# Another written order of 2400 tasks, and four more idle products, in a fused attention and feed-forward kernel

## The chip, the cores and the metric

The kernel runs on one core of a Trainium2 chip. The engines named below are TensorE (PE; its weight loads are listed apart as PEld), VectorE (DVE), ScalarE (ACT), GpSimd (POOL) and SyncE (SP, which only issues transfers here). The metric is device time in microseconds (us), the median of several runs. A profiled execution gives the trace that is quoted; its own time is given beside its span.

## The reference

Two blocks, one after the other. The first is a linear attention with decay (batch 4, 8 heads, 768 steps, 48 channels a head), the second a feed-forward block on 3072 tokens (384 to 2048 to 384):

```python
for t in range(S):
    kt, vt, rt = (k[:, :, t], v[:, :, t], r[:, :, t])
    cur = np.einsum('bhd,bhe->bhde', u[None] * kt, vt)
    y[:, :, t] = np.einsum('bhd,bhde->bhe', rt, state + cur)
    state = w[None, :, :, None] * state + np.einsum('bhd,bhe->bhde', kt, vt)
...
x = np.ascontiguousarray(attn_out.transpose(0, 2, 1, 3)).reshape(B * S, H * D)
h = x @ w_in
g = h - np.tanh(h)
return (g @ w_out).astype(np.float32)
```

The inputs are float32, but the two weights of the feed-forward block come as 64-bit floats and are converted on the chip.

## The kernel before

**Attention in units.** The 768 steps are cut into 12 chunks of 64, and the four batches into two halves of two; a unit is one chunk of one half, so there are 24 units, numbered chunk by chunk, and unit n needs the state that unit n - 2 left. A unit loads r, k and v (SP, two transfers each; the first two units share them with ACT's queue), transposes r and k on PE into one PSUM tile (L806 and L808: `turn`, `turn_k`), scales them (`rT` on DVE, L660; `kT` on ACT, L692, or on DVE), forms the scores (`lev`, L828, 32 or 64 small products), masks them on DVE (`cp`, L830), adds the diagonal (`rk`, `rk` times u, `du` on DVE, then `diag` on ACT in two halves; for unit 0 alone the diagonal is a product of its own with `kU` and `w_u`), multiplies with v (`out`, L831) and updates the state (`add`, L792, and `decay`). The result goes through ACT to `xt` and `rest` (L765); POOL then issues six small transfers that move `rest` into the free rows of `xt`. Units 0 and 1 have `extra`, a copy on POOL (L739), in its place. Units 12 to 23 take r and k already spread out by SP and transpose them on DVE.

**The feed-forward block in tiles.** Two units make one block of 256 tokens (j = 0 to 11), and 256 columns of w_in make one tile, named j.f with f = 0, 2, ... 14: 96 tiles. A tile is a first layer of two halves on PE (L217; two h buffers in PSUM), five ACT steps (`s` arctan L229, `th` and `tg` tanh L231 and L233, `sq` L224, `small` L235), three DVE steps (`g`, `m`, `cp`, L242 to L246), and a second layer in two halves: plain products (L254) for the first tiles of blocks 0 to 5 and the very last tile, and else seven products of half size in place of eight (L307), for which POOL, or DVE in two of the last tiles, forms three sums of g (L290 to L294). PE runs first layers ahead of second layers by several tiles.

**Weights.** 16 pieces; each is loaded in parts (SP and POOL for w_in, SP for w_out) and converted by five DVE and two ACT instructions (cv0.0 to cv0.6 for piece 0, L185 to L191).

**The order.** The whole program is a list of 2400 tasks with their dependences, made by `add(engine, cost, run, after, ...)`. Which task is written when is not computed: it is read from the string ORDER, two characters of a 64-letter alphabet a task. Each engine and each DMA queue works in the order in which its tasks are written. The numbers from 2400 on stand for idle products, whose result nothing reads, and for the reading of a flag:

```python
idle, done = [run for _, _, runs in self.fills for _, run in runs], set()
for n in (DIGITS.index(x) * len(DIGITS) + DIGITS.index(y) for x, y in zip(ORDER[::2], ORDER[1::2])):
    if n < len(self.tasks):
        t = self.tasks[n]
        assert all(x.n in done for x in t.after)
        done.add(n)
        yield t.run
    else:
        yield (idle + [None])[n - len(self.tasks)]
```

Idle products (L534) come in four kinds: 512 or 256 columns wide ("wide", "narrow"), into an h buffer or into the PSUM tile of the early units' transposes. They multiply the identity with itself. Nothing else in the program depends on ORDER; the costs and due times given to `add` are not used when the order is read from the string.

Of the kernel before, what the change touches and what calls it, by code (L numbers as in the profile page):

```python
# [42 lines left out]

DIGITS = "0123456789ABCDEFGHIJKLMNOPQRSTUVWXYZabcdefghijklmnopqrstuvwxyz+_"
ORDER = (
    "00010J2i2j2k2f2g2h0H2m2l2nbWbW020K030I040605bWbX2q3435362o3231330A2s0F0B0C2r2ubWbX2x072v2y082w2t0T092z0L380M3U3C"
# [4 lines left out]
    "5Q6A8q8Y56696B5R8Z5S5t5A6c578f5E5u5m8g5B5Y8i5v5lba5n595p8j5C8a585D6Z8b5Z8t0u6a6b8k8s5o5w8l6d6e5a8m8c6F5q5b6J8n14"
    "6N6G6H5r5c6O738o5s775d5x8w74755y6P8r8u915z6Q5e76786n8v6K6f8x5+6R6g6h6o6p6I5_926L7T8y7U7V609D7X6M67617W7Y6q6j656S"
    "7H636r0v687A668z6T956494936i98966U7IJx9762JyJz6k7J6V9EJ+6l6W8+J_K06m6X797B9G996s1D9H7h129F6Y9I9A9R907D7K6tKP9S9K"
    "7L7a9L6u9T7i9U7j0G7C0x9J7E6vKL9d7FKMKN0y8_7Z7b7d9e6w9MKOKQ9V726x9B7G6_1L9Y7k6z707M0zK16+719f9C7N9W9h9Z7c9X7e9iKs"
    "9a7O7lKu16K9K2K39N7PKAKvKw6y9O7g7fKrKt7QKZKa9r0+7RKR179g0_7m9Q9P9j9k9b187n10197o119s7p9l1T1U1E9c1F7q1A1G7vA19m7t"
    "9v1B7u1H7xA21C7w9u7y9t9n9yA41e1fKB1V9w1W1I1gKC1h9oLF1JA5LGLHAF9x1M9p1NA3AGA81O9z9qAR9+KDA6ASA7A9AJKb9_AIAAAUAMA0"
    "1PKc1QABAH1RAKAfAL1SATAg1iAVANAWAYAXAC1jADAZ1kArK6AEAaLIAhAsKWAi1xAOAkLJLKAjAPLl1lAmLmLnAnAQAuAvAtAyB3Aw1mAlB4Az"
    "AxLo1KLpLqAbB51XB6AoBFA+B71YB8BABG1Z1n1aBT1oBIBJBBAc2G2HBHL31p2FB9L4BUAdBMBKBCBf1bBWAeL5BVAp1cBYBXBNBgBLBaBbAqBi"
    "LTBh1dA_7S23241q2526B01rMABO1sKSKTB1BtBk1yBj1z1tBuB2Bm1+1uBD1_1vBZBE1wBlBvBcBPBy20KxBxBQBwKyKzBnBz2PB_2EC327B+28"
    "C4Bo29BRCH2A21C7BSCIC52BC6C0BdCK22CJCACLBe2XC82CM9MBCMCTCOC92ICN2DBp2J2QBq2RBr2SCUCPMf2TLzMgMhCBChCWCCCVBsCYCiCQ"  # L60
    "CXKdCbC1N3L+CZN4N52UC2CkCj2VCmCDCl2W2KCaCE2LCoCnCt2M2NCuCcD5CFCxCpCwCvCqD6CyCGC+CRD82OD7CzDK2Y2Z2aDL2bCSD92cDADC"
    "CdDBDDC_DZCfDM2dDNCe2eDaCgDECrD0DcDODFCsDbDRDGDdDPDgDoDQ85De86DpDfDS7rD1DrDhDq87EEDTD3DsDUDiEFDtDVDvD2EHDH81DuDW"
    "89ETEIDjEGELEJEUD4DkEK88EiDwEW8AEVDxDIEXEYDJDXEaDy7sDlEjEMENExEk8BElLUEmEy8CEZLVEnEbDYEoEqEzDmEpEOEcEPFNErE_DzE+"
    "FOF0EQF1D+F3DnFQ82FPD_F2EdFSE1EeFTE2FcF4EfFRE3E4E0FdE5EsE6EtE7ERE8FeEBFfE9FUFhESEuFVFgEDFrECFWF5FjEgF6FsEhFtFvEv"
    "FwFXFuFzFYFiEw7zFxEAG4FyF7FZFkG5Fl83F8FmG684G9FnG8F9F+G7FAGWGB7+FBGXFCFDFEFaFFGYGaFGFKGbGlGCGAFLGZF_FbGdFoGmGeGD"
    "FpFHGnFIGqG0G+GoGcG1FMGpG_GfGE7_FqGFH2GsH0FJG280H1GgGtGrG3GGH3H4GhGHGiGJGKGIGLGMHDGNGOGPHEGQGTGSH6GjK5GuH5HHGvGk"
    "HFH7GwHIHfHGGxHJHKH8HgK4H9GVGyHiHAHhHkGzHjHBHlHnHLKVHuK8HvHmK7I7HxHwI8HMKUHyHNHCH_IAHOHzHPHQH+I0HoKEI1IBHpI9IEIM"
    "ICHqKYGRINHrIFLPGUIoKFIOIQKXIDKGIRIPHRIUL6ITIpK+IGISHSIHKHJ1HTHUIIIVI2KIJ2HVIqKJIJIrHsHWL7HXK_HYHtJ4IsKeJ5IWIvIt"
    "IXIuJGKfI3J3I4L1J6I5LOJ7HZIwJHHbJ8HaIxI6JIL2JLKgJJLuJKKKL0JVLWHcJNJMHeJWJ9IyKhJAIKHdKiLQLMJOLXILKmLvKjIzJZL_IZI+"
    "JYJPIYIbJXIcIaJBJaIdIeJbKpL8IfJcKnKlIgI_MCJCIhL9KqMDMEJQIiJ0JRJdJEJSKoLAMNMjJDMOMiMkJFIkLBIlLSJTImLCInLRPJMJKkPK"  # L70
    "JeMtJfPYPLPNJgPMJUIjPOMIPQJhPZPPPRLDLEPnPaPbPcPoPfLLLNPSLYPqNaMuPrPTNZNbQ0M0PuPULZM1PVQ1MPLxPpPdJiN+PsPgLrPeQFQ3"
    "PhJkQ2JlLaPiQ4JmJnPtPjQ7JjLbLyQGLcJoMpMKQUPvLfQILkPwQHQ5QVPxQJQ8Q6LgPWJpLjQWPyJqQKQMLsLtLhPXQXJrPkMoQLLdPlQZJuQ9"
    "M2LwQYQAMQPmQBMLQaJwP+MRPzMFQbJtN6M3QjLiNzN_MMMGMHM4QcN7N8LeQkM5MqQNQyQmQOQlQPQnQzNcM6QqQQQdQRP_M7R0QCRMQ+JsQ_Qe"
    "QoR3MSJvM8QfRNMsQgQDMvNjMTMwMrQEMxMUQrQpRPQsRbR1QtR2R4NiQSRQQuR5QvQTRTRcR6R7QhReR8NDRORRQiRSRUQwRfRVRdRiRgQxRWRh"
    "RXRqMmRYNdNeRrMlMnS3RsRuRtS4O1MVRxN9RjR9NANBRkNCRBRCSIS7RlRDS5RERvRAS8S6RZMWSARFRwO0O2SJRyNfRGRzNgNhSXRHSMR+NESK"
    "SYRLSLMbS9SPR_RaSBS0MXSmSZMZMYSNMcSCSaRoMdSOSQRJSDSRMyMeRINHSnRmNnOWRnOTRpSoMaOUOVSbRKS1OXOYScSSSeSpSfSTSrS_MzSq"
    "SESdSuSFOrS2SsStSUNFSGSvT0O6NINJTPT1NoT2NpSHSgNGShM+SiTQM_O7SjSVTST3TRSWT6TTT4SkTWNKOBT7NLSlNkOvT5TeTUOsOtT8N0O4"
    "TfTXT9NqOhTtTATVN1SwTiTYTuThTBTgTlTjSxSzTkSyTmTwNMTnTxT+U6U7S+U9UATCTvToUDU8TZNmTyULTaTzT_UBOdUMTbU0TpUaNNUOUNUC"
    "TDTEUQTFUbU1TGO3O5THU2OuOwTITcUdTMUPURUSNOOCTJUpNPTKODTONlTdNQU3OEUqNWN2OcNVUTTqTrUENTP3UcNRTsNrUUU4UFOFNSUVUfOi"
    "U5UsUWUrNsUeUGUtUhTLUJUgNtUHUuUIV2UvUXUxTNOANUUKNXNYV3O9UYUiO+P4UwNuUjUyVSNvOjUzUZV4U+OkUkOaUnO_V6UlOlUmVTU_V5V7"  # L80
    "UoV8VAV0VWV9VVVUOZObVhVZVXVBVYVaViNwVbVwVjVcOxVkOyOzVCVlVxVdVoVeOeV1VDV+NxVyVFVEVzVmVnVpOGV_W0W2W9VHW1VGW3O8WAVI"
    "VJOHWOVqNyWDVrOgOIWCWBP5WPVKVLVMVfVOWQVNW4WEOJVgW5WHVsVuOfOKVtWSORVvWGP6OOOLOQWdP7OMVQP0VRWTW7OPWRW6WFW8WIWeWVWJ"
    "WKOmWfOSWgWLWhVPWsP1WtOnP2OoWvWkWMOpWWWNWUOqWXX5WuWYWwP8WiWZWzWjWaONX6WxP9WlWbX8WmWyW+WnX9PAX7XCW_WcPBXVPCXAXWPD"
    "PIPFXkXYWoXZPHXBWpXlXcPEXXXDX0XzXnXaWqXbXdXEWrXoXFXmX3XGXpX1XqXsXHX+XrX2XtPGYCY0XeX_Y2XfX4Y1YDY4XuY5XgXIYGXvYFXh"
    "XKYRYJYEXwYHY3XJYKYIXLYSXMXNYLXiY6YTYVY7YgYUYWYYYXXOYhXPXSXQXRYvY8YjXTYkY9YiXjYlXxYmYnYMYZXUYwYNYaYOYoXyYxYzYpZ8"
    "YyYbZ0Z9YcYdYAZBY+ZCZYZ1ZAZDYBY_ZZZFYqZ2YrZnZGZcYsZbYPZEZaZHZdYQZeZoZfZ3Z4YeZpZ5ZqZrYfZsa0ZtZuZIZvZJYtZwZgYuZhZ6"
    "Zia1aFa2a5aGa4a3a6a7Z7aJa8aIaUZxaMZyZLZzZKZNZjZOaVa9ZkZPZMZQaXaHZlZRaAaKZSaLZVaNajaYZUaOaWaBabaZakaCZTZWZmalanZ+"
    "aaaPamZXayaQaqaRacazadbIa+b0a_Z_bJb3aeafaDagbLaoapaEarb1asaSb2bKaTbNbMahbObPb4aib5atawb6aubQavaxb7bRb9b8bBbCbAbD"
    "bEbSbFbGbHbUbTbV"
# [1190 lines left out]
```

## Time and profile before

| what | value |
|---|---|
| time, median of 3 runs (lowest to highest) | 581.05 us (579.9 to 581.28) |
| profiled execution | 582.91 us, its span 581.2 us |
| busy: PE, DVE, ACT, POOL | 563.5, 432.1, 404.1, 202.5 us |
| granted TensorE clock, mean | 0.994 |
| first-layer products, L217 | 1152 passes, 269.0 us busy |
| second-layer products, L307 and L254 | 994 and 200 passes |
| bytes moved | 38.48 MB, most of it in the first 120 us |

A busy PE in this profile is a PE with a pass under way; the ends of passes are modelled, and a float32 product is recorded as two passes. Idle time is put down to the engine or transfer whose semaphore came last before the instruction. Times in rows are from the start of the span.

### The profile page before, as it was taken

The page shows a single profiled execution, that of the slowest core. Times are in us where ns is not written, and L with a number is a line of the kernel's source. Part 1 is how long each engine was busy: PE and PEld are TensorE (multiplying, and loading weights), DVE is VectorE, ACT ScalarE, POOL GpSimd, SP SyncE. Part 2 cuts the span into 40 slices and gives each one's busy share as a digit, 9 for nine tenths or more (in the row PEclk, how much of TensorE's full clock was granted, in tenths as well). Part 3 has the DMA queues.
Part 4 walks back from the last instruction along what each step waited for, and adds up shares of the span by engine and source line. Part 5 has one row for each costly group of instructions (what it writes and reads, how often), then busy time and mean ns, then how long its engine had stood idle before and what let it go on. Part 6 is the DMA issues. An engine that isn't in the chain of part 4 may idle for free.

```text
span 581.2 us, 14164 instructions
## 1 busy us (share of the span) xinstructions
PE 563.5 (97%) x5487; PEld 481.5 (83%) x5487; DVE 432.1 (74%) x720; ACT 404.1 (70%) x926; POOL 202.5 (35%) x366
## 2 busy tenths in 40 slices
...
GB/s 130 162 204 137 125 100 189 103 76 167 114 120 15 1 1 12 17 55 41 40 74 86 62 94 39 72 86 39 25 50 60 16 34 7 3 29 2 14 16 32
DMA packets 138548, 38.48 MB, mean 66 GB/s; under 512 B 130760, under 2 KB 132904, under 8 KB 138472
## 3 DMA queue, kind: packets, MB, share of 16 engines
...
q14 instruction: 31, 0.25, 0.1%
...
## 4 chain that ended last, share of the span: by engine, by line
PE 79%; DMA 1%; ACT 1%; POOL 0%; DVE 0%; issue 0%; DVEq 0%; POOLq 0%
PE h L217 39%; PE p L307 28%; PE o L254 7%; PE yk_ps L606 5%; DMA xt<-rest 1%; PE p L254 0%; ACT xt L765 0%; POOL xt L786 0%; ACT rest L765 0%; ACT kT L692 0%; DVE rk L696 0%; DVE state L792 0%; DVE last L265 0%; PE x_ps L606 0%; DVEq L696 0%
## 5 line engine op out<-in xcount | busy, mean ns | idle before, releaser
L217 PE MATMUL h<-xt,w_in_sb 128*128 128x256 f32 x1152 | 269.0, 381 | 0.4 <-DMA xt<-rest 0.2
L217 PEld LDWEIGHTS h<-xt,w_in_sb 128*128 128x128 f32 x1152 | 214.8, 190 | 33.1 <-DVE w_in_sb L191 0.9
L290 POOL TENSOR_TENSOR sg<-g 128x256 f32<-128x256 f32 x69 | 55.9, 811 | 200.8 <-DVE g L246 147.0
L242 DVE TENSOR_TENSOR g<-h,th 128x512 f32<-128x512 f32 x96 | 65.8, 686 | 61.8 <-ACT tg L233 20.7
L229 ACT ACTIVATE s<-h 128x512 f32<-128x512 f32 x96 | 57.1, 595 | 54.5 <-PE h L217 40.0
L244 DVE TENSOR_TENSOR tg<-s,tg 128x512 f32<-128x512 f32 x96 | 71.7, 751 | 31.2 <-ACT s L224 27.7
L307 PE MATMUL p<-mixed,sg 128*128 128x192 f32 x426 | 93.0, 327 | 0.0
L246 DVE COPY_PREDICATED g<-small,tg 128x512 f32<-128x512 int32 x96 | 74.3, 783 | 12.6 <-ACT small L235 9.9
L231 ACT ACTIVATE th<-h 128x512 f32<-128x512 f32 x96 | 56.8, 593 | 35.0 <-PE h L217 34.7
L307 PEld LDWEIGHTS p<-mixed,sg 128*128 128x128 f32 x426 | 73.5, 190 | 1.4
L233 ACT ACTIVATE tg<-h 128x512 f32<-128x512 f32 x96 | 56.6, 592 | 22.9 <-DVE g L246 13.3
L307 PE MATMUL p<-w_out_sb,g 128*128 128x192 f32 x284 | 69.9, 328 | 0.0
L235 ACT ACTIVATE small<-s,smallb 128x512 f32<-128x512 f32 x96 | 68.5, 720 | 1.2
L254 PE MATMUL o<-w_out_sb,g 128*128 128x384 f32 x192 | 67.2, 489 | 0.1
L224 ACT ACTIVATE s<-s 128x512 f32<-128x512 f32 x96 | 60.1, 630 | 1.1
L786 POOL DMA_DIRECT2D xt<-rest x66 | 32.6, 498 | 68.9 <-ACT rest L765 68.4
L307 PEld LDWEIGHTS p<-w_out_sb,g 128*128 128x128 f32 x284 | 51.1, 190 | 2.7
L254 PEld LDWEIGHTS o<-w_out_sb,g 128*128 128x128 f32 x192 | 35.9, 190 | 19.4 <-issue 0.2
L704 ACT ACTIVATE at<-same,du 128x64 f32<-128x64 f32 x184 | 47.7, 340 | 5.0 <-DVE du L700 4.8
L292 POOL TENSOR_TENSOR sg<-sg,g 128x128 f32<-128x128 f32 x69 | 39.9, 581 | 3.6
L294 POOL TENSOR_TENSOR sg<-sg,g 128x128 f32<-128x128 f32 x69 | 38.1, 559 | 3.0
L307 PE MATMUL p<-w_out_sb,sg 128*128 128x192 f32 x142 | 34.9, 328 | 0.0
...
## 6 DMA issues: line engine op xcount, KB each, us to landing
...
```

The lines of the kernel that those rows point to most:

```text
L217: self.nc.tensor.matmul(t.h2[:, z], self.w_in_sb[:, t.f // 2, kk, z * 128 : (z + 1) * 128], self.xts[t.j][:, kk].rearrange("p b t -> p (b ...
L224: A.activation(t.s, t.s, AF.Square, scale=G3)
L229: A.activation(out, t.h, AF.Arctan, scale=G2)
L231: A.activation(out, t.h, AF.Tanh)
L233: A.activation(out, t.h, AF.Tanh, scale=G1)
L235: A.activation(out, t.s, AF.Relu, bias=self.smallb, scale=-1.0)
L242: V.tensor_tensor(t.g, t.h, t.th, ALU.subtract)
L244: V.tensor_tensor(t.tg, t.s, t.tg, ALU.mult)
L246: V.copy_predicated(t.g, t.small.bitcast(I32), t.tg)
L254: self.nc.tensor.matmul(self.outs[i], t.g2[:, z, i * C : (i + 1) * C], self.w_out_sb[:, t.f + z, :], start=t.first and z == 0, stop=t.last ...
L290: add(t.s4[:, :2], g[:, 0::3], g[:, 1:2].to_broadcast([128, 2, C]), ALU.add)
L307: self.nc.tensor.matmul(ps[bank][:, half * n : (half + 1) * n], a, b, start=t.first and half == 0, stop=t.last, skip_group_check=True)
```

## The change

ORDER is replaced as a whole. The tasks, their dependences, tiles and buffers are the same 2400. The string has 2420 entries in place of 2416: three more wide idle products (one into an h buffer, two into the transposes' tile) and one more narrow one (into an h buffer), 19 in place of 15. On each engine part of the tasks change place: PE 273 of 462 (by at most 8 places), ACT 514 of 653 (at most 35), DVE 551 of 688 (at most 35), POOL 290 of 337 (at most 16), SP 136 of 188 (at most 30).

The head of the diff:

```diff
 ORDER = (
-    "00010J2i2j2k2f2g2h0H2m2l2nbWbW020K030I040605bWbX2q3435362o3231330A2s0F0B0C2r2ubWbX2x072v2y082w2t0T092z0L380M3U3C"
-    "2+2p0N37393A3G2_3V3W0O3E0U3H3S3I3B3J3D3R3T3F0P3KbWbWbX3L0V3u3b300S3MbX3c3v3w0Q3N3a3f3s3O3g3P3r3t3e0R3Y3Q3hbX8D0w"
...
+    "00010J2f2g2h2i2j2k2l2m2n0HbWbW020K030I040605bWbW2obX2q3534363231332s2t2r070F0A383739bWbX2x0B0C2u082y09bX2v0LbX3C"
+    "3B3U0M3V3W2w0N0U2pbW2z3R0O3G3A3H2+3I2_3F3S3T0V3E3J0T3D3u3K0PbW3L3v3w3b303MbX3c0S0Q3N3r3f3a3s3t3O3g3e3P0R3Y3Q3h3X"
...
 )
```

Decoded and split by engine, the first stretch reads as follows (- before, + after). Names in brackets carry the unit or the tile j.f; ha and hb are the halves of a first layer, oa and ob of a plain second layer, pa and pb of one with seven products; fill is an idle product into an h buffer, xfill into the transposes' tile (w wide, n narrow); state is the state's product of units 0 and 1; rku is rk times u; dga and dgb are the halves of the diagonal; W1.2 is part 2 of weight piece 1, k3.1 the second transfer of unit 3's k, st and xt the transfers out and into xt.

```
PE   -: fill.w fill.w cols fill.w fill.n turn_k(0) turn(0) fill.w fill.n lev(0) own(0) table out(0) turn_k(1)
        turn(1) state(0) fill.w fill.w fill.n lev(1) fill.n turn_k(2) out(1) turn(2) state(1) fill.n ha(0.0)
        lev(2) hb(0.0) turn_k(3) out(2) bound turn(3) xfill.w ha(0.2) lev(3) xfill.w out(3) turn_k(4) turn(4)
        hb(0.2) xfill.n lev(4) xfill.n turn(5) out(4) turn_k(5) oa(0.0) ob(0.0)
PE   +: fill.w fill.w cols fill.w fill.w turn(0) fill.n turn_k(0) fill.w fill.n lev(0) table fill.n own(0)
        fill.n turn_k(1) fill.w out(0) turn(1) state(0) fill.w lev(1) fill.n turn_k(2) out(1) turn(2) state(1)
        fill.n ha(0.0) lev(2) hb(0.0) turn(3) bound out(2) turn_k(3) xfill.w xfill.w xfill.w xfill.n lev(3)
        ha(0.2) out(3) turn(4) turn_k(4) hb(0.2) xfill.n lev(4) xfill.w out(4) turn_k(5) turn(5) oa(0.0)
        ob(0.0)
ACT  -: rows k0.1 r0.1 v0.1 ups k1.1 r1.1 keeps kU(0) doubled downs v1.1 xt(0) cv0.2 cv0.3 dga(1) dgb(1)
        add(0) xt(1) kT(2) add(1) dga(2) dgb(2) cv1.2 cv1.3 s(0.0) dga(3) xt(2) kT(3) rest(2) dgb(3) tg(0.0)
        cv2.2 cv2.3 sq(0.0) dga(4) xt(3) rest(3) kT(4)
ACT  +: rows r0.1 k0.1 v0.1 ups k1.1 r1.1 doubled keeps v1.1 kU(0) downs cv0.2 cv0.3 xt(0) dga(1) dgb(1)
        add(0) xt(1) kT(2) add(1) dga(2) dgb(2) cv1.2 cv1.3 tg(0.0) dga(3) xt(2) kT(3) rest(2) dgb(3) s(0.0)
        cv2.2 cv2.3 sq(0.0) dga(4) xt(3) rest(3) kT(4)
DVE  -: now now now kT(0) rT(0) cp(0) diag(0) cv0.0 cv0.1 kw(0) rk(1) kT(1) rku(1) du(1) kw(1) rT(1) cv0.4
        kw(2) cp(1) cv0.5 rk(2) rku(2) cv0.6 du(2) rT(2) cv1.0 kw(3) cv1.1 rk(3) cp(2) rku(3) du(3) cv1.4
        cv1.5 flagged cv1.6 rT(3) cv2.0 add(2) cv2.1 rk(4) kw(4) rku(4) cp(3) du(4) cv2.4 decay(2) cv2.5 kw(5)
        rT(4) add(3) m(0.0) cv2.6 cp(4) g(0.0) rk(5) cp(0.0)
DVE  +: now now now kT(0) rT(0) cp(0) cv0.0 kw(1) cv0.1 diag(0) kw(0) rk(1) rku(1) du(1) kT(1) rT(1) cv0.4
        kw(2) cp(1) cv0.5 rk(2) rku(2) cv0.6 du(2) rT(2) kw(3) cv1.0 cv1.1 rk(3) cp(2) rku(3) du(3) cv1.4
        cv1.5 rT(3) cv1.6 cv2.0 flagged add(2) cv2.1 rk(4) kw(4) rku(4) cp(3) du(4) cv2.4 cv2.5 decay(2) kw(5)
        rT(4) add(3) cv2.6 m(0.0) cp(4) g(0.0) cp(0.0)
SP   -: rows W0.2 k0.0 r0.0 W0.0 v0.0 k1.0 r1.0 ub k2.0 v1.0 k2.1 W1.2 r2.1 r2.0 k3.0 W1.0 k3.1 r3.1 r3.0 v2.1
        v2.0 k4.1 W2.0 k4.0 r4.0 r4.1 v3.1 v3.0
SP   +: rows W0.2 r0.0 k0.0 v0.0 W0.0 k1.0 r1.0 ub v1.0 k2.0 k2.1 W1.2 r2.0 r2.1 k3.0 k3.1 W1.0 r3.0 r3.1 v2.1
        v2.0 k4.1 W2.0 k4.0 r4.0 r4.1 v3.1 v3.0
POOL -: W0.3 W0.1 w_u now extra(0) W1.1 extra(1) W1.3 W4.3 W5.3 xt xt xt xt xt xt W5.1
POOL +: W0.3 W0.1 extra(0) w_u now extra(1) W1.3 W1.1 W4.3 W5.3 W4.1 xt xt xt xt xt xt W5.1
```

Later places that the text below refers to, again before and after:

```
PE   -: ... ob(5.6) ha(1.10) hb(1.10) ha(1.12) pa(0.8) pb(0.8)    (hb(1.8) stands ahead of ob(5.6))
PE   +: ... ob(5.6) hb(1.8) ha(1.10) hb(1.10) ha(1.12) pa(0.8) pb(0.8)
PE   -: ... hb(11.10) pb(11.0) pa(11.2) ha(11.12) hb(11.12) ha(11.14) pb(11.2) hb(11.14) pa(11.4) pb(11.4) ...
PE   +: ... hb(11.10) pb(11.0) ha(11.12) hb(11.12) pa(11.2) pb(11.2) ha(11.14) pa(11.4) hb(11.14) pb(11.4) ...
DVE  -: ... rku(11) du(11) cv4.0 rT(10) cv4.1 kw(11) cp(2.2) add(9) g(3.0) cp(10) m(3.0) cp(3.0) cv5.0 ...
DVE  +: ... rku(11) du(11) kw(11) cv4.0 cv4.1 m(2.2) cv5.0 rT(10) add(9) rk(12) decay(9) cp(10) cp(2.2) ...
```

The end of PE's list, from pa(11.6) on, is the same in both.

More of the change, by code (lines that the diff above doesn't have):

```diff
@@ L45 @@
 ORDER = (
-    "00010J2i2j2k2f2g2h0H2m2l2nbWbW020K030I040605bWbX2q3435362o3231330A2s0F0B0C2r2ubWbX2x072v2y082w2t0T092z0L380M3U3C"
-    "2+2p0N37393A3G2_3V3W0O3E0U3H3S3I3B3J3D3R3T3F0P3KbWbWbX3L0V3u3b300S3MbX3c3v3w0Q3N3a3f3s3O3g3P3r3t3e0R3Y3Q3hbX8D0w"
-    "3d3i0W3k3X3Z3_3j0X4P430Y8E0d3l4O4Q0Z444L40458F4M4N3m0a463y0D0b3+3n0E0c423o41bY8P150e473x3z3p4p0f8H484Z4o4q0g4V4a"
-    "0h494l8I4bbY4A4R0i4c4m4n4W3q4B4U0j4S4T8Q4v0l4C4X5I4Y4J4D4d8L4K5GbZ4e4I0k5J5K8R4F8G5F5H4f4H8J4G8KbZ4u8S134g4z8U8M"
-    "8T4+4w4s4h0m8N4_4x4i8O4E5i4y4j5j5k500n525P4r4t8V4k5f8d8W515T0t0o5U8e536C0p5V5g5h8p8X5W5M0q6D6E5X540r8h5O0s555L5N"
@@ L51 @@
[L51 to L89, printed above, removed]
+    "00010J2f2g2h2i2j2k2l2m2n0HbWbW020K030I040605bWbW2obX2q3534363231332s2t2r070F0A383739bWbX2x0B0C2u082y09bX2v0LbX3C"
@@ new lines @@
+    "3B3U0M3V3W2w0N0U2pbW2z3R0O3G3A3H2+3I2_3F3S3T0V3E3J0T3D3u3K0PbW3L3v3w3b303MbX3c0S0Q3N3r3f3a3s3t3O3g3e3P0R3Y3Q3h3X"
+    "3ZbX8D0w3d3i3_3k3j0W4P0X8E430d0Y3l4O4Q0Z444L3+454M4N0D8H3m0a463y400b3n41420c3o0e3x3z15470E3p4p0u0fbYbYbYbZ488F4o"
+    "4q4Z0g4V4a8P4m0h494b8I4l4n4A0i4c4S4U0j4B4R4T4W3q8Q5J4v4C4X4Y0l4H4D4d5I5K0k4IbZ4e4K5G8G8L4F5F5H8J4f4J8S4G8KbY4g8T"
+    "138M8R4z4w4h4E4u8N4+4x4i5j0m8O8U4_4r4y4j4s4t500n528X5g515T8d5i5k5U0o535f5h8e0p8W5L5V8V0q8p5M5N8g6D5W0r6C6E545P5X"
+    "8Y695Q550s5O6A6B8q5m5R564k5t8Z5l5n5S5C578h6d5E5u8f5B6Z5p5Y8i5D8k8j5A6cba6e5v8a595Z5w6G8l6a6b8b5a8m8t148c5o5b6J6F"
@@ new lines @@
+    "6H5q6N768n585s5r5c738o8s77785d5x6O5y8w8r6P74758u915z6f6Q8x6g6h8v5e5+6n7X6R8y6K7W7Y5_6I926L7U606o7T7V9D6p796M6461"
+    "94666j6q6S65J+676r7A7B688z6T63J_K093620t966U0v95976k7D6V6i7Z989E6l7a7b6W7HJy8+129F6XKO999I9R6m7I9G7J9A7K6sJxJz6Y"
+    "7h0GKPKQ7L9S6t1D8_9H7E9U6u9K9T7i907C7j9W9d7d9VKL0x6vK10y9B9LK2K36w16KMKN9e7F7G727k6x6z1LK96+7M6y7l70719C9J7N6_9X"
+    "9M7O0z9Y9Z0+7e7c7P9N7fKr9a7QKu9OKAKvKw9g0_9PKsKt9f9rKB7g7R9QKZ9h7m1710189b7n19Ka9i117o9j1A1U9s7p1W9k1B9c7q9l9t7u"
+    "A11E9w7t9m9x7w1F7xA29vKb7v1G1C7y9n9u1M1e1f1H1g1N1h9oA41V9yLFA51I9pAF1T1OA8KS9zA3KRKTAG1P9+A6AR1QA7A99qASKCAALGLH"
@@ new lines @@
+    "1RAH9_AJL3AK1SAIA0AV1J1xAT7SABKDAM1iAUAfAW1jANADKx1kAgAYLmALLlLnACAXAOAi1KAjAr1l1X1pAZAhAsAmAk1mKcB3AaAtAnAEB4Aw"
+    "1YAlKWAPL4AuAv1ZAQAy1aAbAx1bB6BFAzB5AoB8BG1nB7B9A+AcBIBABJAdBTBMBHBBBKBUBCBL1cBfBV1dAeBWBg1oBXBYL52FApK6BZ2H1qBi"
+    "LI26BNAqLJLK241r25Bb1s23A_BO2GBhBa2EBjB01tB1Bm1yBt1zB21+Bu1u1_1vBDBvBcBk20BEByBx1wBlC3BnBw2P27LpC421LoLqBoM9BP28"
+    "MAMBB+29BQB_2ACHBz2BC6BRC7CIBS2CBdCKC0LTCLBe22C5C8CA2XBpC9MgCOCJMfMh2DBqCM2ICNCPCT2J2QCU2RCQ2SLzCh2KBrN3Bs2TCiCB"
+    "KyKzN4N5CCCVC12UCXCW2VC2Ck2LL+CaCDCl2WCYCjCECoCm2MCZCtCpCn2NCu2OD5CGCwCFKdCbCRCcCvCy2YD62ZCqCSD8CxCzC+CdD9C_2aDK"
```

28 lines of the change are left out of this document (added).

## The prediction

> **What bounds the kernel now.** I read the page first, then busy time by stage, then the waits of TensorE, then single engines in order of time where something waits. The page begins:
>
> ```profile
> span 581.2 us, 14164 instructions
> ```
>
> Cut where the character of the work changes, the stage table (span, then busy time of PE, PEld, DVE, ACT, POOL, then granted clock, DMA share, GB/s) is:
>
> ```profile
> 0.00:33.50 33.50, 26.20 (x451) 17.42 (x451) 21.91 (x42) 15.64 (x40) 9.81 (x39) 0.95 0.94 158
> 33.50:50.00 16.50, 13.31 (x310) 9.53 (x302) 14.38 (x25) 15.62 (x47) 3.43 (x7) 1.00 0.78 166
> 50.00:117.00 67.00, 65.83 (x1112) 49.66 (x1110) 58.68 (x101) 64.19 (x184) 14.13 (x29) 1.00 0.66 132
> 117.00:573.00 456.00, 455.75 (x3625) 403.79 (x3625) 335.18 (x552) 308.67 (x658) 175.12 (x291) 1.00 0.25 46
> ```
>
> Four stages, four limits. Up to 33.5 us loads set the pace (DMA share 0.94) and PE is padded with idle products. From 33.5 to 50 ScalarE does: 15.62 of 16.50 us. From 50 to 117 PE (65.83 of 67.00) and ACT (64.19) are both nearly closed. From 117 to 573 PE idles 0.25 us in 456. So the last and by far the longest stage has nothing to give: another order of the same matmuls can only open a gap there. What an order can win lies before 117 us and in the tail. The two rows at the head of PE's waits (total, number, longest):
>
> ```profile
> PE yk_ps L606 <- DVE state L792: 2.0, 2, 1.7
> PE x_ps L656 <- issue: 1.6, 2, 0.8
> ```
>
> The largest single one, 1.7 us, is for the state update of unit 2. "issue" is a wait for nothing that the profile shows; no order aims at it.
>
> **Part 1, before 33.5 us: the loads and POOL's queue.** In the new order POOL takes `w_u` (L564) after `extra` of unit 0 (L739), and one load of weight piece 1 goes behind `extra` of unit 1. POOL, then ACT, in order of time:
>
> ```profile
> 8.46 0.20 POOL L564 TENSOR_TENSOR w_u<-saved 128x4 f32<-128x4 f32 x1 [1.84 <-ACT saved L563]
> ...
> 12.81 0.26 POOL L739 COPY extra<-vt 128x96 f32<-128x96 f32 x1 [2.90 <-DMA vt<-in_v_dram]
> ...
> 20.20 0.26 POOL L739 COPY extra<-vt 128x96 f32<-128x96 f32 x1 [6.43 <-DMA vt<-in_v_dram]
> ```
>
> ```profile
> 9.90 1.28 ACT L709 ACTIVATE kU<-kT,w_u 128x128 f32<-128x128 f32 x4 [1.59 <-DVE kT L665]
> ```
>
> POOL works in order, so `w_u` now waits for v of unit 0. If v lands as before, `kU` starts at 12.81 + 0.26 + 0.20 = 13.3 instead of 9.9: 3.4 us late, and behind it in ACT's queue are w_down and the first xt, and on DVE the diagonal of unit 0 and both kw. v is issued one place earlier on SP, which can take part of this back. The cover lies in waits of DVE that follow:
>
> ```profile
> DVE rk L824 <- DMA ub<-in_u_dram: 1.1, 1, 1.1
> DVE power L185 <- DMA st<-in_moe_w_in_dram: 1.0, 1, 1.0
> DVE smallb L1233 <- PEq L1263: 0.9, 1, 0.9
> DVE kw L807 <- issue: 0.8, 1, 0.8
> DVE rk L696 <- DMA rt<-in_r_dram: 0.8, 1, 0.8
> ```
>
> Without the one of smallb, which comes before all this, they sum to 1.1 + 1.0 + 0.8 + 0.8 = 3.7 us, more than 3.4. The load that moves back on POOL goes out just behind the 20.20 row, one issue later than the load of the same piece that stands there already; kw of unit 3 now comes ahead of that piece's conversion and uses its wait of 1.0 us. I take 0. Bounds: +3.4 with no cover; -1.7, if the clock that this stage lost (0.05 of 33.5 us) is all kept and all on the path. The order of PE changes too (transposes and idle products between the first two units), inside the same waits.
>
> [...]
>
> **Part 2, the idle products.** 19 in place of 15: three wide (512 columns) and one narrow (256) more. PE around unit 3's scores:
>
> ```profile
> 33.73 0.66 PE L656 MATMUL x_ps<-ident,rt 128*128 128x128 f32 x4
> 34.22 1.02 PE L534 MATMUL x_ps<-ident 128*128 128x512 f32 x2
> ...
> 38.59 0.69 PE L606 MATMUL yk_ps<-rT,state 48*64 48x64 f32 x32 [1.69 <-DVE state L792]
> ...
> 50.21 2.75 PE L254 MATMUL o<-w_out_sb,g 128*128 128x384 f32 x8
> ```
>
> A wide one takes 1.02 us, a narrow one no more: 3.1 to 4.1 us of PE time if nothing hides it. What hides it: the waits for loads in the first 20 us, and the 1.69 us here, where three wide and one narrow in a row now stand in place of one wide and the first half of a dense tile. Without that cover it costs all 3.1 to 4.1. I take 0 on top of part 3.
>
> **Part 3, 33.5 to 50 us: the table load and the chain to unit 3's scores.** ACT, then DVE:
>
> ```profile
> 32.25 1.28 ACT L229 ACT_TABLE_LOAD   x1 [1.86 <-PE h L217]
> 33.54 0.60 ACT L229 ACTIVATE s<-h 128x512 f32<-128x512 f32 x1
> ...
> 36.77 0.86 ACT L765 COPY rest<-yk_ps 64x64 f32<-64x64 f32 x4
> ...
> 39.11 0.92 ACT L187 ACTIVATE power<-power,p_bias 128x768 uint32<-128x768 uint32 x1
> ```
>
> ```profile
> 34.32 0.96 DVE L191 TENSOR_TENSOR w_in_sb<-w_in_sb,power 128x768 f32<-128x768 f32 x1
> 36.91 0.69 DVE L660 TENSOR_TENSOR rT<-x_ps,power 128x512 f32<-128x512 f32 x1 [1.63 <-ACT kT L692]
> ...
> 37.98 0.55 DVE L792 TENSOR_TENSOR state<-yk_ps,state 128x384 f32<-128x384 f32 x1
> ```
>
> rT of unit 3 waits 1.63 us until ACT's kT, written ahead of it and reading the same PSUM tile, has ended. In the new order rT is written first and can run when its transposes are done, at about 34.4. ACT's first function of a dense tile becomes tg (tanh) instead of s (arctan); the table load at 32.25 stands directly ahead of the first arctan. If the table already loaded serves tanh, tg starts at 32.25, rest of unit 2 ends at 32.25 + (36.77 + 0.86 - 33.54) = 36.3 instead of 37.6, and the state update follows at about 36.7 instead of 37.98. The four idle products run from 33.73 + 0.66 = 34.4 to 37.5 or 38.5, say 38.0, and are then what the scores wait for: some 0.6 us earlier than 38.59.
>
> Most of it does not stay. The load only moves behind the second half of unit 3's diagonal, where s now is. From the start of s to the conversion at 39.11 are 5.57 us of gapless ACT work; 32.25 + 5.57 + 1.28 = 39.1 in either order, and ACT is closed after it. What can remain is the idle time that ACT still has in this stage, 16.50 - 15.62 = 0.9 us. I take -0.25, nearer to nothing than to all of it. Bounds: 0, and -1.1 if PE carries the stage (1.69 less 0.6).
>
> [...]
>
> **Part 4, 50 to 117 us.** Both engines closed, the same work. PE idles 67.00 - 65.83 = 1.2 us, of which an order may win all or add as much. 0, bounds -1.2 and +1.2.
>
> **Part 5, 117 to 573 us.** The visits of PE to attention work are as many as before, 24. What costs is a dense tile whose first layer follows the one two before it with a single first layer between, since there are two h buffers. Before has one such place; PE, then ACT:
>
> ```profile
> 489.78 6.90 PE L217 MATMUL h<-xt,w_in_sb 128*128 128x256 f32 x30
> ```
>
> ```profile
> 494.47 0.60 ACT L229 ACTIVATE s<-h 128x512 f32<-128x512 f32 x1 [0.20 <-DVE g L242]
> ```
>
> 30 passes take 6.90 us from the first start to the last end. s ends at 495.07, 5.3 us after that start; by then, at 6.90 / 30 = 0.23 us a pass, 23 passes have gone, and the next tile's come right after it. So PE waited here by a fraction of ACT's 0.20; I price the place at 0.25 us. The new order has three (tiles 1.8, 6.14, 10.4): +0.5, and since in two of them ACT takes th, tg and s in one row, I take +0.25. Bounds 0 and several times that, since the stage has no other reserve.
>
> **Part 6, the tail.** DVE, then PE's weight load:
>
> ```profile
> 569.60 0.28 DVE L294 TENSOR_TENSOR sg<-sg,g 128x128 f32<-128x128 f32 x1
> ...
> 569.94 0.30 PEld L307 LDWEIGHTS p<-w_out_sb,sg 128*128 128x128 f32 x2 [0.24 <-DVE sg L294]
> ```
>
> The three sums of that tile (11.10) now come ahead of the next tile's instead of alternating with them. I take -0.2; bounds -0.24 and +0.6, as the last tile's first layer comes one half (1.3 us) later against the end.
>
> **Sum.** 0 + 0 - 0.25 + 0 + 0.25 - 0.2 = -0.2 us. The profiled execution took 582.91 us, 1.7 of it around the span of 581.2; in its terms 582.7. The median of the runs shown, 581.05, is 1.86 below the profiled one; in its terms 580.85, and I say 580.9. About 0.3% (1.74 us) is what a measurement of this kernel can tell from no change.
>
> **Rivals.** *The early gain stays* (faster). The scores of unit 3 come up to 1.1 us earlier, ACT makes room because its order meets PE's better, the 1.2 us of part 4 go too, and the tail gives 0.2: 581.05 - 2.5 = 578.55. For it: DVE's wait of 1.63 us comes from the written order alone and goes; against it: ACT closed from 33.5 to 117. Chance 0.34.
>
> *The late stage spends its reserve* (slower). With PE at 455.75 of 456, any place where a first layer follows too closely on a used buffer opens a gap that nothing gives back. At 0.25 us each it decides from seven such places; ten give 581.05 + 2.5 = 583.55. For it: the old order met hardly any gap in this execution; against it: I find three tight places among 96 tiles. Chance 0.17.
>
> *POOL's queue is not covered* (slower). 3.4 us less only the 1.1 us wait for ub: 583.35. It decides when the weights and r that DVE waits for come early. Chance 0.09.
>
> *The reordered tanh costs a third table load*: if the table taken for tanh lacks arctan, ACT pays 1.28 us more in a closed stage: 582.3, within the bound. Chance 0.04.
>
> The forecast, no change that can be told: 0.36, its own range 579.3 to 582.8. Faster 0.34, within 0.3% 0.36 + 0.04 = 0.40, slower 0.17 + 0.09 = 0.26. The range, 577.8 to 584.3, reaches 0.75 us past either rival's time (the bounds of parts 1 and 5 go farther) and leaves about 2 in 10 out.
>
> **What would show it.** Right: rT of unit 3 without a wait for kT; the table load directly ahead of an arctan and behind unit 3's diagonal; unit 3's scores at 37.5 to 38.5; the first second-layer product, at 50.21 before, within 0.5 us of that; PE idle under 1 us from 117 to 573. Wrong: that product more than 1.5 us from its place (parts 1 to 3), or PE idle of 2 us or more in the long stage (part 5).

## The result

The changed kernel takes 586.31 us (median; 585.52 to 586.87) beside 580.47 us (579.02 to 581.28) for the kernel before in the same comparison: a ratio of 1.0102 with a 95% interval of 1.0077 to 1.0128. Compared again on another occasion it was 587.38 beside 580.25, 1.0122 (1.0092 to 1.0153). The forecast was 580.9, no change. The profiled execution of the changed kernel took 586.87 us, its span is 585.2 us, against 582.91 and 581.2 before. The spans are thus 4.0 us apart where the medians are 5.8: the profiled execution of before was 2.4 us above its median, and a dip of its clock, told of further down, is about 1.7 of that.

PE's waits on the page's waits view (total, number, longest) put the loss in one place. The first three rows after:

```profile
PE h L217 <- DMA xt<-rest: 4.0, 2, 2.1
PE yk_ps L606 <- issue: 1.8, 1, 1.8
PE yk_ps L606 <- DVE state L792: 1.6, 1, 1.6
```

A wait of PE for the small transfers from `rest` to `xt` was 0.2 us before. In the changed kernel this is the chain of waits from 107 us on (start, duration, what; the view ends at 125 us and cuts its last piece there):

```profile
107.79 0.23 ACT rest L765
108.01 0.28 issue
108.29 2.12 POOL xt L786 x4
110.41 7.64 DMA xt<-rest
118.05 0.14 issue
118.19 6.82 PE h L217 x18
```

POOL issues the six transfers of tile block 5 at once when ACT has written `rest`, but the one that PE waits for needs 7.64 us to land. The median over the whole kernel (row of L786, issue to landing, minimum, median, maximum) is nearly the same before and after, and the longest differs; before, then after:

```profile
DMA to landing us min/median/max: 1.6/2.2/5.7
```

```profile
DMA to landing us min/median/max: 1.6/2.3/7.8
```

PE in order of time around the first tile of block 5 (tile 5.0), before and then after:

```profile
113.47 2.74 PE L254 MATMUL o<-w_out_sb,g 128*128 128x384 f32 x8
116.05 1.03 PE L217 MATMUL h<-xt,w_in_sb 128*128 128x256 f32 x4
117.32 4.55 PE L217 MATMUL h<-xt,w_in_sb 128*128 128x256 f32 x20 [0.25 <-DMA xt<-rest]
121.71 4.03 PE L254 MATMUL o<-w_out_sb,g 128*128 128x384 f32 x12
```

```profile
110.73 2.75 PE L254 MATMUL o<-w_out_sb,g 128*128 128x384 f32 x8
115.43 0.67 PE L217 MATMUL h<-xt,w_in_sb 128*128 128x256 f32 x2 [1.95 <-DMA xt<-rest]
118.19 7.68 PE L217 MATMUL h<-xt,w_in_sb 128*128 128x256 f32 x22 [2.09 <-DMA xt<-rest]
125.70 4.03 PE L254 MATMUL o<-w_out_sb,g 128*128 128x384 f32 x12
```

Ahead of tile 5.0 the new order is 113.47 - 110.73 = 2.74 us ahead; behind it, it is 125.70 - 121.71 = 3.99 us late. Of this swing of 6.73 us, 1.95 + 2.09 - 0.25 = 3.79 are the waits. Nearly all of the rest is speed: the same 24 passes take 0.67 + 7.68 = 8.35 us in place of 1.03 + 4.55 = 5.58, which is 2.77 us more. The table by stage shows why, before and after. Its last three columns are the granted clock, the DMA share (the time that packets took, as a share of the core's 16 DMA engines) and GB/s:

```profile
112.00:118.00 6.00, 5.75 (x23) 4.04 (x22) 5.56 (x8) 5.79 (x15) 3.11 (x7) 1.00 0.72 148
118.00:124.00 6.00, 6.00 (x26) 4.61 (x26) 4.65 (x8) 5.97 (x15) 0.00 (x0) 1.00 0.70 100
```

```profile
112.00:118.00 6.00, 2.15 (x7) 0.87 (x5) 5.45 (x9) 5.97 (x12) 0.42 (x1) 0.90 1.19 177
118.00:124.00 6.00, 5.82 (x15) 4.67 (x16) 4.02 (x6) 1.85 (x6) 0.00 (x0) 0.53 0.77 188
```

The clock fell while PE stood still and stayed low when it went on: in slices of 1 us it is 1.00 up to 116 us, 0.91 in the next, 0.50 in the six from 117 to 123, and 0.68 in the one after. PE works again from 118.19; the 4.81 us up to 123 at 0.50 and the next at 0.68 come to 4.81 x 0.50 + 0.32 = 2.7 us of full speed lost, which accounts for the 2.77. The DMA engines were at 1.19 in place of 0.72. The rest of the span adds little: the last products of the kernel start at 572.65 and 577.13,

```profile
572.65 2.74 PE L254 MATMUL p<-w_out_sb,g 128*128 128x384 f32 x8
```

```profile
577.13 2.74 PE L254 MATMUL p<-w_out_sb,g 128*128 128x384 f32 x8
```

4.48 us apart, so 0.49 us were lost after tile 5.0, and from there to the end of the span it is 8.55 us before and 8.07 after. -2.74 + 6.73 + 0.49 - 0.48 = 4.0, the difference of the spans.

**What fills the DMA engines.** SP's queue, before and after (issue times; the transfers to `st` are weight loads of 288 KB each):

```profile
112.85 1.28 SPq L171 DMA_DIRECT2D st<-in_moe_w_in_dram  x3
```

```profile
107.75 1.29 SPq L171 DMA_DIRECT2D st<-in_moe_w_in_dram  x3
109.09 0.60 SPq L644 DMA_DIRECT2D rt<-in_r_dram  x1
109.74 0.62 SPq L171 DMA_DIRECT2D st<-in_moe_w_in_dram  x1
```

POOL's, before and after:

```profile
110.67 2.89 POOL L786 DMA_DIRECT2D xt<-rest  x6 [1.65 <-ACT rest L765]
```

```profile
108.29 3.08 POOL L786 DMA_DIRECT2D xt<-rest  x6 [3.25 <-ACT rest L765]
```

Before, one load of piece 8 goes out at 107.97 and the other three (pieces 8 and 9) from 112.85 on, behind five of the six small transfers; the sixth, the one that PE waited 0.25 us for, took 4.11 us to land. After, all four, 1.15 MB, go out from 107.75 to 110.36, ahead of and among them. A load of piece 9 waits for the staging buffer that the sixth conversion step of piece 5 (cv5.5, L190) frees; the two rows are of DVE, before and after:

```profile
111.84 0.94 DVE L190 SCALAR_TENSOR_TENSOR power<-st,power 128x768 uint32<-128x768 uint32 x1
```

```profile
106.75 0.94 DVE L190 SCALAR_TENSOR_TENSOR power<-st,power 128x768 uint32<-128x768 uint32 x1
```

111.84 + 0.94 = 112.78 and 106.75 + 0.94 = 107.69, each less than 0.1 us ahead of its load. In the string the loads of piece 9 stand behind the small transfers in both orders. That binds nothing here: they are on different queues, and the two times just given show SP going when its buffer is free.

### The profile page after: what moved, and what is told of

Its sections match the earlier page's. It is cut to its first block, busy times and chain, and to the rows that moved or that the text cites. A ratio compares the mean times of both kernels' runs of the same rounds, so it can differ in the third digit from the quotient of the medians.

```text
span 585.2 us, 14166 instructions
## 1 busy us (share of the span) xinstructions
PE 569.6 (97%) x5495; PEld 484.6 (83%) x5495; DVE 432.9 (74%) x720; ACT 404.9 (69%) x926; POOL 204.1 (35%) x366
## 4 chain that ended last, share of the span: by engine, by line
PE 80%; ACT 7%; DVE 5%; DMA 4%; issue 2%; POOL 1%; ACTq 0%; DVEq 0%; POOLq 0%
PE h L217 39%; PE p L307 27%; PE o L254 7%; PE yk_ps L606 5%; DMA xt<-rest 2%; DMA rt<-in_r_dram 2%; ACT at L704 1%; ACT xt L765 1%; ACT rest L765 1%; POOL xt L786 1%; PE h L534 1%; DVE tg L244 1%; PE x_ps L656 0%; DVE g L242 0%; PE p L254 0%
## 5 line engine op out<-in xcount | busy, mean ns | idle before, releaser
L217 PEld LDWEIGHTS h<-xt,w_in_sb 128*128 128x128 f32 x1152 | 217.4, 192 | 37.1 <-issue 2.6
L290 POOL TENSOR_TENSOR sg<-g 128x256 f32<-128x256 f32 x69 | 54.7, 795 | 189.2 <-DVE g L246 134.7
L244 DVE TENSOR_TENSOR tg<-s,tg 128x512 f32<-128x512 f32 x96 | 69.9, 731 | 35.1 <-ACT s L224 20.5
L786 POOL DMA_DIRECT2D xt<-rest x66 | 32.6, 498 | 79.6 <-ACT rest L765 79.3
L292 POOL TENSOR_TENSOR sg<-sg,g 128x128 f32<-128x128 f32 x69 | 42.6, 620 | 3.2
L294 POOL TENSOR_TENSOR sg<-sg,g 128x128 f32<-128x128 f32 x69 | 38.5, 563 | 3.7
L307 PE MATMUL p<-mixed,g 128*128 128x192 f32 x142 | 34.8, 327 | 0.1
```

The source lines that it names most:

```text
L217: self.nc.tensor.matmul(t.h2[:, z], self.w_in_sb[:, t.f // 2, kk, z * 128 : (z + 1) * 128], self.xts[t.j][:, kk].rearrange("p b t -> p (b ...
L244: V.tensor_tensor(t.tg, t.s, t.tg, ALU.mult)
L290: add(t.s4[:, :2], g[:, 0::3], g[:, 1:2].to_broadcast([128, 2, C]), ALU.add)
L307: self.nc.tensor.matmul(ps[bank][:, half * n : (half + 1) * n], a, b, start=t.first and half == 0, stop=t.last, skip_group_check=True)
```

## The experiments

Times are medians, beside the kernel before in the same comparison (579.63, 580.25, 580.64 and 580.99 us in the four groups); ratios carry their 95% interval. Edits are given as differences of an engine's list, in the names of the change.

### Is it the loads? Taking them away from the changed kernel

e1_w9_later and e2_w8_first leave every instruction of the engines where the changed kernel has it and move only loads on SP:

```diff
 SP  r14.1
-W9.0 W9.2
 W8.2 r15.0 W8.0 v13.1 v13.0 r15.1 W11.0
+W9.0 W9.2
 v14.0
```

```diff
 SP  r14.1
+W8.2 W8.0
 W9.0 W9.2
-W8.2
 r15.0
-W8.0
 v13.1
```

> The changed kernel with two entries of SP's list moved: the two large loads of weight piece 9 go behind the load of piece 11, so those of piece 8 go out some 4 us earlier and those of piece 9 behind the six transfers of tile 5's rest. Theory C (the loads of pieces 8 and 9, 1.15 MB issued at 107.75 to 110.36, crowd out the small transfers that move rest into xt): these transfers land within about 2.5 us of their issue, PE's two waits of 1.95 and 2.09 us ahead of tile 5 and the clock dip after them go, 586.3 - 6.7 = 579.6 us (579.0 to 580.5). Rival L (the new order lets PE reach tile 5 too soon after its transfers are issued, whatever else moves): waits and time stay, 586.3.

> The changed kernel with the two large loads of weight piece 8 written ahead of those of piece 9 on SP, nothing else. Piece 8 then goes out when its staging buffer is free, about 103.4, and only piece 9 (0.58 MB instead of 1.15) stands at 107.75, ahead of the six transfers. Theory C: about half of the delay is left, PE waits 0.5 to 2 us ahead of tile 5, 580 to 583.5 us. Rival L: 586.3.

e1: 585.7 beside 579.63, 1.0092 (1.0056 to 1.0127). The total was missed by 6 us, but not for the reason that rival L gave: the waits for xt are gone. PE's and DVE's waits in it have another name:

```profile
PE h L217 <- DVE g L242: 3.6, 2, 3.3
```

```profile
DVE power L185 <- DMA st<-in_moe_w_in_dram: 5.2, 1, 5.2
```

The conversion of piece 9 stands on DVE where it stood; its load now comes 13 us later, DVE waits 5.2 us in front of it, and the `g` behind it in DVE's queue holds up PE. I had moved the transfer and not asked who waits for it.

e2: 582.35, 1.0038 (1.0010 to 1.0065), inside the expected 580 to 583.5: with half of the bytes ahead of the small transfers about two thirds of the loss is gone. Its profile has a wait for xt of 0.8 us, but it is of the fastest of twelve executions, at a clock of 1.000 where their median is 0.996, so it need not be typical.

e5_no_block adds to e1 the other half of the move, on DVE. On ACT it also moves the third step of the same conversion (cv9.2) four places back, behind the two tanh of tile 0.4:

```diff
 DVE decay(10) g(5.0)
-cv9.0 cv9.1
 m(5.0) g(5.2) cp(5.0) cv6.6 cv8.0
+cv9.0 cv9.1
 m(5.2) g(0.4)
-cv9.4
 cp(5.2) m(0.4) cv8.1 kw(13) rku(14)
+cv9.4
```

> The changed kernel with the loads of piece 9 behind that of piece 11, as in the first experiment, and with the first two conversion steps of piece 9 on DVE behind the first step of piece 8 (and its fifth step three places later), so that DVE does not stand before a load that has not landed. Theory C+ (the loss is the collision at tile 5 plus the clock dip that PE's standing still brings, and the new order is otherwise even with the old one): neither the wait for xt nor the wait for g, 578.5 to 580 us beside a kernel before of about 579.6. Rival M (part of the loss sits in the rest of the new order): 581.5 or more.

582.96 beside 580.25, 1.0034 (1.0016 to 1.0053). The two thirds of the loss are gone again, yet 2.7 us stay (2.0 by the ratio): too much for C+, and what M expected. Part of it can be named, and it is of my making, not the new order's: DVE still waits 1.06 us for the load of piece 9, and PE 2.1 us for `g`:

```profile
PE h L217 <- DVE g L242: 2.1, 2, 1.8
```

### Putting the stall into the kernel before

e3_before_w9_early moves two conversion steps on DVE, which frees piece 9's buffer early:

```diff
 DVE cp(11) cv4.5
+cv5.4 cv5.5
 cv4.6 m(3.2) cv6.0 cv6.1
-cv5.4
 cp(3.2)
-cv5.5
 cv5.6 g(4.0)
```

> The kernel before with two DVE instructions moved: the fifth and sixth steps of the conversion of piece 5 come right behind the sixth step of piece 4, so the staging buffer of piece 9 is free at about 109.8 instead of 112.8 and its loads go out ahead of and among the six transfers of tile 5's rest (issued from 110.7) instead of behind them. Theory C: the stall appears in the kernel before: 580.5 + 4 to 6.7 = 584.5 to 587 us, with a PE wait for xt of 2 us or more near 116. Rival L: 580.5, no such wait.

585.36 beside 579.63, 1.0092 (1.0064 to 1.0121). Two instructions of one engine, moved by five places at most, cost as much as the whole change. SP now issues four loads in one row ahead of the small transfers, PE waits 2.1 us, and a transfer takes up to 6.5 us to land:

```profile
104.42 3.46 SPq L171 DMA_DIRECT2D st<-in_moe_w_in_dram  x4
```

```profile
PE h L217 <- DMA xt<-rest: 2.1, 1, 2.1
```

Rival L falls: PE is ready for tile 5.0 at 112.67, 5.5 us after the first of its transfers is issued (107.13); before it was 116.05 - 110.67 = 5.4 us.

### The clock's share

```diff
             t.h = t.h2.rearrange("p z t -> p (z t)")
+        for _ in range(10 if (t.j, t.f, z) == (5, 0, 0) else 0):
+            self.nc.tensor.matmul(t.h2[:, z], self.w_in_sb[:, 0, 0, :128],
+                                  self.xts[t.j - 1][:, 0].rearrange("p b t -> p (b t)"), start=True, stop=True)
         for kk in range(d.NK):
```

> The changed kernel with ten idle products (0.43 us each, 4.3 us) ahead of tile 5's first product, into the h buffer that it is about to fill; they take the place of the two waits of 1.95 and 2.09 us. If the clock of 0.5 to 0.8 from 115 to 124 us is a consequence of PE standing still, it stays at 1.00 and the 2.7 us that it cost go: about 583.6 us. If the dip has another cause, 586.3.

584.32 beside 579.63, 1.0075 (1.0049 to 1.0101); the changed kernel stands at 1.0102 and 1.0122, so 0.27 to 0.47% (1.6 to 2.7 us) are back, although PE does 4.3 us of products for nothing (from 111.59 to 115.91 in its profile). The intervals of the ratios overlap, so the size of this gain is only roughly known. The mean clocks do not overlap: 0.996 to 0.999 in its eight executions, 0.987 to 0.994 in the changed kernel's nine. Behind the idle products PE still waits 1.1 us for xt. In its profile the clock stays at 1.00 through the stall:

```profile
112.00:118.00 6.00, 4.93 (x23) 4.05 (x22) 5.43 (x9) 5.00 (x11) 0.00 (x0) 1.00 1.11 158
118.00:124.00 6.00, 6.00 (x27) 4.80 (x26) 4.26 (x8) 3.50 (x8) 0.00 (x0) 1.00 0.89 251
```

### Three thirds of the order

The list was cut at the first second-layer product (about 50 us) and at the first layer of tile 0.4 (about 125 us); each stretch is taken from one order, the tasks left over in the relative order of the other.

```diff
 e6_early_only    -old       +new to 50 us,         old from there
 e9_middle_only   -old       +old to 50 us, new to 125 us, old from there
 e7_late_only     -old       +old to 125 us,        new from there
 e8_middle_old    -new       +new to 50 us, old to 125 us, new from there
```

> The new order up to the first second-layer product of tile 0.0 (about 50 us, all 19 idle products in it), then all other tasks in the relative order of the kernel before. Theory C+: even with the kernel before or up to 1.5 us faster, 578 to 580 us (579.6 beside it). Rival E (the 1.7 us that the two traces show at that product is a lasting gain of the new order): 577.9 or less. Rival M: the early part costs, 581 or more.

> The kernel before up to the first layer of tile 0.4 (about 125 us), then all other tasks in the relative order of the new one. Theory C+ and the forecast's parts 5 and 6 (+0.25 and -0.2): 579.6 to 580.3 us beside 579.6. Rival M (the tight places of the long stage spend more than was priced): 581.5 or more.

> The changed kernel as it is, as the reference for the runs beside it. Theory C+: a loss of 4 us of waits for xt ahead of tile 5 and one clock dip in nearly every execution: 5.5 to 6 us over the kernel before, mean clock 0.992 to 0.995. If the collision depends on how the transfers happen to fall in an execution: executions of 580 to 582 us at a clock of 0.998 or more turn up among them.

> The changed kernel with only its middle taken back: the new order up to the first second-layer product (about 50 us), the old relative order from there to the first layer of tile 0.4 (about 125 us), the new order for the rest. Theory C+ (the loss arises in the middle, at tile 5): the two waits for xt go, 580 to 582.5 us, since the late part alone gave 581.8 and the early part 580.75. If the loss needs the new order on both sides: 584 or more stays.

> The kernel before with only the middle of the new order, from 50 to 125 us. Theory C+: the two waits for xt of some 2 us each and the clock dip behind them, 585 to 587.5 us beside 580.3. If the collision depends on the early part having moved PE ahead: 580 to 582.

| kernel | us | beside | ratio (95%) | PE's wait for xt, us |
|---|---|---|---|---|
| e6, early new | 580.75 | 580.25 | 1.0000 (0.9979 to 1.0021) | 0.2 |
| e9, middle new | 587.55 | 580.64 | 1.0105 (1.0076 to 1.0134) | 4.2 |
| e7, late new | 581.83 | 580.25 | 1.0037 (1.0011 to 1.0063) | 0.2 |
| e8, middle old | 581.95 | 580.64 | 1.0017 (0.9998 to 1.0035) | 0.2 |
| changed, again | 587.38 | 580.25 | 1.0122 (1.0092 to 1.0153) | 4.1 |

The middle alone makes the loss, with the same two waits (e9):

```profile
PE h L217 <- DMA xt<-rest: 4.2, 2, 2.1
```

It does not need the early part. The second profile of the changed kernel has 4.1 us of it as well; no execution of it came near 580. e7 is the miss here: 1.6 us above the kernel before beside it (2.1 by the ratio), where 0 to 0.7 was expected, about the 1.9 (581.5 - 579.6) that rival M asked for. In it and in e8, which share their second seam, PE waits 0.65 us for `g` at 129 to 130 us, a wait that neither whole order has; how much of the 0.37% the seam makes, and how much the late part, stays open. The three thirds add up to 1.42%, more than the 1.02 and 1.22% of the whole, and e8, with the early and the late part both new, has 0.17%; so the late part of the whole change may cost less than e7 says.

### The early part: idle products and ACT's queue

e10_early_15_idle and e11_idle_unit4 start from e6, on PE's list:

```diff
 PE  own(0)
-fill.n
 turn_k(1)
-fill.w
 out(0)
...
 turn_k(3)
-xfill.w xfill.w
 xfill.w xfill.n lev(3)
```

```diff
 PE  hb(0.2)
-xfill.n
+xfill.w xfill.w
 lev(4)
```

> The early-only kernel (580.75 us) without the four idle products that the change adds: a wide one ahead of unit 0's outputs, a narrow one ahead of unit 1's transposes, two of the three wide ones ahead of unit 3's scores. Forecast's part 2 (hidden in waits, worth nothing by themselves): 580.3 to 581.2. If they cost their 3.1 to 4.1 us: 577 to 578. If they hold the clock up: more executions with a dip ahead of 40 us, 582 or more.

> The early-only kernel with two wide idle products in place of one narrow ahead of unit 4's scores, where PE waits 1.6 us for unit 2's state and where three of its kin showed the clock dip (0.91 from 40 to 60 us). If the dip follows from that standing still: fewer dips, mean clock nearer 0.998 than 0.995, 579 to 579.5 us, ahead of the kernel before. If it follows from something else: 580.75 or 0.2 us more.

e10: 580.67 beside 580.64, 0.9998 (0.9977 to 1.0020): the four idle products are worth nothing in time, as part 2 had it. Yet the mean granted clock of its executions is lower, 0.9915 against 0.995 for e6 (medians of twelve). In its profile the clock is 0.79 from 10 to 20 us and 0.87 from 20 to 30, beside DMA shares of 1.28 and 1.07. So early, the slower clock does not show in the time; that waits for loads hide it is my guess, which no run shows. e11: 579.84 beside 580.64, 0.9972 (0.9952 to 0.9992), ahead of both kernels. The waits for the state fall from 2.2 us in e6 to 0.9, but the clock's median stays at 0.995, so the gain can't be put down to the clock: that step of the expectation was wrong.

e12_v_behind_kU (from e11) and e13_before_v_ahead (from the kernel before), on ACT's list:

```diff
 ACT doubled keeps
+kU(0)
 v1.1
-kU(0)
 downs
```

```diff
 ACT keeps
+v1.1
 kU(0) doubled downs
-v1.1
 xt(0)
```

> The early-only kernel with idle products at unit 4 (579.84 us, 0.28% ahead of the kernel before), and on ACT's list the transfer of v of unit 1 goes behind kU of unit 0 instead of ahead of it. In the new order ACT stands before that transfer until 12.50 us and kU starts 2.1 us after its inputs are there; PE waits 0.8 to 2.2 us for kU. If this wait is on the path: kU at about 11.1, no wait of PE for kU, 0.5 to 2 us less than 579.8, that is 577.8 to 579.3. If it is covered by the later waits for loads, as the forecast's part 1 had it of POOL's queue: 579.8.

> The kernel before with one task moved: the transfer of v of unit 1 on ACT's queue ahead of kU of unit 0, as in the new order. If the wait is on the path: kU some 2 to 3 us later, 580.6 + 0.5 to 2 = 581.1 to 582.6 us. If it is covered: 580.6.

The reason for the pair is this stretch of ACT in the changed kernel:

```profile
12.50 0.61 ACTq L644 DMA_DIRECT2D vt<-in_v_dram  x1
13.22 1.28 ACT L709 ACTIVATE kU<-kT,w_u 128x128 f32<-128x128 f32 x4 [3.04 <-DVE power L185]
```

and POOL ahead of it:

```profile
10.65 0.26 POOL L739 COPY extra<-vt 128x96 f32<-128x96 f32 x1 [4.05 <-DMA vt<-in_v_dram]
10.88 0.20 POOL L564 TENSOR_TENSOR w_u<-saved 128x4 f32<-128x4 f32 x1
```

`w_u` is ready at 11.08, but ACT stands before a transfer until 12.50. Moved behind kU, kU starts at 10.68 in e12 and PE no longer waits for it (1.9 us in e11); 579.52 beside 580.99, 0.9976 (0.9950 to 1.0003), clock 0.999 (median of twelve). That is 0.0004 from e11's ratio, so no gain that can be told. e13 moves kU from 9.90 to 12.02 and measures 1.0003 (0.9979 to 1.0026): covered.

## Why the prediction was wrong

**The step that failed is part 4.** "Both engines closed, the same work" priced 50 to 117 us by what PE idles, at 0 with bounds of -1.2 and +1.2 us. The middle alone is worth 1.05%, 0.0105 x 580.64 = 6.1 us. Part 4 looked at engines and not at queues: SP's list is moved by up to 30 places, DVE's by up to 35, and nothing in it asks when a moved conversion frees a buffer, which load that releases, and what else is on the way then. The sign was in the trace of before: four loads of 288 KB, and a tile that already waited 0.25 us for its last small transfer (the row at 117.32), so that any later landing had to show. No rival held it either; the one rival of a queue was about POOL in the first 15 us.

**Part 1** (0; +3.4 to -1.7): right in size, 0.03% +- 0.24% in e13. That a late `kU` is covered is shown there for 2.1 us; which later waits cover it is not. The mechanism was read on the wrong queue, and that `kU` starts at 13.22, where 13.3 was forecast, is luck. POOL had `w_u` at 11.08, because v landed 2 us earlier; the 2 us came from ACT, whose own transfer was written ahead of kU, an entry that the prediction's text did not follow.

**Part 2** (0): right. With the four idle products the early part stands at 1.0000 (e6), without them at 0.9998 (e10).

**Part 3** (-0.25): the events came as described. DVE, ACT and PE after:

```profile
33.35 0.69 DVE L660 TENSOR_TENSOR rT<-x_ps,power 128x512 f32<-128x512 f32 x1
```

```profile
31.13 0.60 ACT L233 ACTIVATE tg<-h 128x512 f32<-128x512 f32 x1 [2.38 <-PE h L217]
...
36.57 1.28 ACT L229 ACT_TABLE_LOAD   x1
37.86 0.60 ACT L229 ACTIVATE s<-h 128x512 f32<-128x512 f32 x1
```

```profile
36.25 0.69 PE L606 MATMUL yk_ps<-rT,state 48*64 48x64 f32 x32
...
44.34 0.69 PE L606 MATMUL yk_ps<-rT,state 48*64 48x64 f32 x32 [1.61 <-DVE state L792]
...
48.49 2.75 PE L254 MATMUL o<-w_out_sb,g 128*128 128x384 f32 x8
```

rT of unit 3 does not wait for kT, the table load stands behind the diagonal and ahead of the arctan, and a tanh runs ahead of it without one, so the third load of the last rival does not exist: the whole trace has two, at 8.21 and 36.57 us (6.84 and 32.25 before). Unit 3's scores start at 36.25 (38.59 before; forecast 37.5 to 38.5). Of these 2.34 us, 1.58 were there before this stage, as told next; the 0.76 left are near the 0.6 that part 3 gave them. Then the gain goes: unit 4's scores wait 1.61 us for a state, almost the 1.69 us that unit 3's waited before. The prediction let the gain end in a closed ACT; where the stall would show next it did not name.

The first second-layer product comes at 48.49, 1.72 us ahead of its 50.21, more than the 1.5 us that were to prove parts 1 to 3 wrong. But 1.58 us of that are there already at the first product of tile 0.0 (24.85 in place of 26.43), about what the clock cost before: from 20 to 24 us (before, then after)

```profile
20.00:24.00 4.00, 3.10 (x58) 2.35 (x54) 3.17 (x7) 1.18 (x6) 1.72 (x4) 0.69 1.17 180
```

```profile
20.00:24.00 4.00, 3.94 (x123) 2.99 (x122) 3.97 (x7) 2.56 (x10) 0.75 (x2) 1.00 1.10 184
```

That is the clock and not the order. Of the kernels that share the early part of before, e7 and e3 show no dip in that stretch (1.00 from 20 to 40 us in e7, from 16 to 33.5 in e3) and start this product at 24.94 and 25.05; e9 has one (0.83 from 20 to 30 us) and starts it at 26.69. The second profile of the changed kernel has a dip ahead of 20 us (0.91 from 0 to 20) and starts it at 26.50. And the early part as a whole is worth 0.0% +- 0.2% (e6). So the rival "the early gain stays" was true of these two traces up to 112 us, and false on average.

**Parts 5 and 6** (+0.25, -0.2): in the traces +0.49 and -0.48. In the row of the long stage

```profile
117.00:573.00 456.00, 454.69 (x3599) 401.95 (x3600) 331.21 (x538) 306.62 (x655) 176.66 (x291) 0.99 0.24 45
```

PE idles 1.31 us; 118.19 - 117 = 1.19 of it are the end of the stall at tile 5.0, so the rest is as a right forecast was to show it. The late part alone measured +0.37%, against +0.01%; with the seam in it, part 5's size stays unsettled, and no reserve of ten places was spent.

A wait of PE and a dip of the clock did not always go together. The wait for the state ahead of unit 4, 1.59 us in the profile of e6 and 1.62 in the second one of the changed kernel, is followed by a dip in the one and not in the other (40 to 60 us):

```profile
40.00:60.00 20.00, 18.41 (x315) 14.21 (x314) 18.76 (x33) 18.39 (x58) 3.44 (x7) 0.91 0.67 140
```

```profile
40.00:60.00 20.00, 18.38 (x323) 14.25 (x321) 19.61 (x34) 19.61 (x63) 3.68 (x8) 1.00 0.63 136
```

In e6 this wait of 1.59 us, up to 43.33, is PE's only one between 38 and 52 us, and the clock behind it is 0.76 from 44 to 46 us, 0.50 from 46 to 48 and 0.89 from 48 to 50. What decides between a dip and none, these runs do not show.
